# A fused pooled attention and SiLU MLP on one core: a fourth seven-product unit per tile, written into one ordered program

## The chip, the cores and the metric

The kernel runs on one core of a Trainium2 chip. A core has engines that work side by side, each taking its own queue of instructions in order: TensorE (PE in the profile; its weight loads stand apart as PEld), VectorE (DVE), ScalarE (ACT), GpSimd (POOL) and SyncE (SP, which here only issues DMAs). They wait for each other through semaphores. PE writes to PSUM[...]; all other tiles lie in SBUF.

The metric is the device time of one execution in microseconds (us). Of the kernel before there are three timed runs, and one profiled execution whose trace all the views come from.

## What is computed

For 8 batches, 8 heads, 576 positions and head size 64, k and v are averaged over groups of 8 positions, so that each head has 72 keys; q attends to them. The result, 4608 tokens x 512 features, is the input of an MLP with 2048 hidden features.

```python
k_p = k.reshape(B, H, Sp, pool, D).mean(axis=3)
v_p = v.reshape(B, H, Sp, pool, D).mean(axis=3)
scores = scale * np.matmul(q, k_p.transpose(0, 1, 3, 2))
attn = np.exp(scores - max); attn = attn / np.sum(attn, axis=-1)
x = np.matmul(attn, v_p)         # to (4608, 512)
h = x @ w_in                     # (4608, 2048)
g = h * (1.0 / (1.0 + np.exp(-h)))
return g @ w_out                 # (4608, 512)
```

## The kernel before

**Tiles.** The MLP works on 9 tiles t = 0 to 8 of 512 tokens. Each has an up phase (x to h, through SiLU, into h_T: 16 groups g of 128 hidden features x 512 tokens, in bf16) and a down phase (h_T to the output). Attention for batch a = t + 1 (576 tokens) is woven into the phases of tile t, so tiles 0 to 6 carry attention and tiles 7 and 8 don't. x goes to xT, a ring of 2304 tokens: tile 4 crosses its end.

**Plain groups.** plain() (L537, L543) makes one group g with four matmuls over 512 tokens into a bank hp_ps, and ACT applies SiLU on the way to h_T.

**Seven-product units.** A unit y makes four groups at once, as a 2 x 2 block product (two pairs of groups, two halves of 256 tokens) in seven block products instead of eight. UNITS lists the pairs of groups: (4, 6), (8, 10), (12, 14). Each product (L477) is four matmuls of 256 columns. The products are called 2, 5, 1, 4, 3, 7, 6. Products 2, 4 and 7 add up in bank P, 5, 3 and 6 in bank Q, 1 is alone in R. Between them stand (in stage()):

- after 2, ACT copies P to r_sb (L494); after 5, DVE adds Q and r_sb to rr_sb (L497); after 1, DVE subtracts rr_sb from R to t_sb (L500)
- after 4 and after 3, ACT applies SiLU straight from P and from Q (L485)
- after 7, DVE adds P and t_sb to c_sb[0] (L509); after 6, Q and t_sb to c_sb[1] (L512); the stages "h" and "s" are ACT's SiLU of c_sb[0] and c_sb[1] into h_T (L485)

r_sb, rr_sb and t_sb exist once, so the units share them. The products use sums of weight blocks (w_sum1, made once) and of x blocks (x_sum, five DVE additions per tile, L444, made in the down phase of the tile before). In tiles 2 to 8 before the change, groups 4 to 15 are made by the three units and groups 0 to 3 by plain(), in the order of the string THREE, where A is the unit with groups 12 to 15, B that with 4 to 7, C that with 8 to 11.

**Down.** down_quarters() (L645) uses the same scheme once for the whole tile: seven products of 16 matmuls with 256 columns, in banks P, Q, R. Products 2, 5, 1, 7 and 6 take sums of h blocks, h_sum[n] (hidden_sum, DVE, L605), as their stationary operand; products 4 and 3 take h_T itself. A sum's high half needs groups 4 to 7 and 12 to 15, its low half 0 to 3 and 8 to 11. After product 2 ACT copies P to r_sb (L658); after 5 DVE makes rr_sb (L660), after 1 t_sb (L664); 4 is copied by ACT (L666) and 3 by DVE (L671) to o_sb; 7 and 6 are added to t_sb by DVE (L675, L679). Then SP's queue stores o_sb.

**Attention in a tile**: POOL sums k and v rows of batch a (behind a gate that waits for an x sum), PE transposes k (kT_ps), DVE transposes q in four pieces, and for each third of the batch come scores (PE L340, ACT exponential L348), denominators (PE L358, ACT logarithm and exponential L367, L368) and numerators (PE L384, DVE multiply L393 to xT). ACT loads a table set ahead of the exponentials (L400) and another ahead of SiLU (L403).

**Order.** Each engine takes its instructions in the order in which the program issues them. up() and down_quarters() issue the matmuls, and a list of fillers (f_up, f_down) says at which step everything else is put in between (spread()). PSUM: 5 banks of kind "at" (units' P and Q, k transpose, scores, denominators, numerators) and 3 of kind "mm" (units' R, plain groups, the down phase's P, Q, R), each kind handed out in turn.

Of the kernel before, what the change touches and what calls it, by code (L numbers as in the profile page):

```python
# [27 lines left out]
FP32 = mybir.dt.float32  # L28
# [4 lines left out]
ALU = mybir.AluOpType  # L33
# [3 lines left out]
def kernel(  # L37
# [53 lines left out]
    def ps_tile(shape, dtype, tag, name):  # L91
        return psum.tile(shape, dtype, tag=tag, bufs=banks[tag], name=name)
# [24 lines left out]
            singles.tile([128, 5, 2, 256], BF16, name=f"w_sum1{n}") for n in range(2)  # L117
        )
    ]
    x_sum = singles.tile([128, 5, 2, NQ], BF16, name="x_sum")  # L120
    gate = singles.tile([128, 1], BF16, name="gate")
    c_sb = [singles.tile([128, 2, NQ], FP32, name=f"c_sb{n}") for n in range(2)]
# [54 lines left out]
    def load_one(b, name):  # L177
        st = batches.setdefault(b, {})
        raw = raw_tile(f"{name}_raw", H)
        nc.gpsimd.dma_start(out=raw, in_=source(b, name)[:, :, :PH])  # L180
        st[f"{name}_raw"] = raw
# [13 lines left out]
    def behind_x_sums():  # L195
        nc.gpsimd.tensor_copy(out=gate[:1], in_=x_sum[:1, U_XI[6], 0, :1])  # L196

    def pool_k(b):
        pool_rows(kp[:SP], batches[b]["k_raw"])
# [119 lines left out]
    def third(n):  # L319
        return tuple((g, n * QV, (n + 1) * QV) for g in range(2))  # L320
# [78 lines left out]
    def attn_tables():  # L399
        nc.scalar.preload_act_table_set("natural_log_exp_and_others")  # L400
# [13 lines left out]

    UNITS = ((4, 6), (8, 10), (12, 14))
    UW = [
        {
            (i, j): w_in_sb[:, 2 * j : 2 * j + 2, 128 * u : 128 * (u + 2)]  # L420
# [14 lines left out]
    def unit_weight_sum(y, n):  # L435
        a, b = U_W[n]
        nc.vector.tensor_tensor(
            out=w_sum1[y][U_WI[n]], in0=UW[y][a], in1=UW[y][b],
            op=ALU.subtract if n in (6, 7) else ALU.add,
        )  # L440
# [19 lines left out]
    def up(t, fillers, items):  # L460
        step = spread(
            fillers,
            sum(
                KF if len(it) == 3 else 2 * len(it[1].strip("hs")) for it in items
            ),
        )
        ps = {}

        def product(y, n, bank, first):
            if first:  # L470
                tag = "mm" if bank == "R" else "at"
                ps[y, bank] = ps_tile([128, 2, NQ], FP32, tag, f"u_ps{bank}")
            w, x = unit_weights(y, n), unit_x(t, n)
            for u in range(2):
                next(step)
                for kk in range(2):
                    nc.tensor.matmul(  # L477
                        ps[y, bank][:, u, :], lhsT=w[:, kk, 128 * u : 128 * (u + 1)],
                        rhs=x[:, kk, :], start=first and u == 0 and kk == 0,
                        stop=kk == 1, skip_group_check=True,  # L480
                    )

        def hidden(y, i, j, src):
            g = UNITS[y][i]
            nc.scalar.activation(  # L485
                h_T[:, g : g + 2, j * NQ : (j + 1) * NQ], src, func=AF.Silu
            )

        tt = nc.vector.tensor_tensor

        def stage(y, n):
            if n == "2":
                product(y, 2, "P", True)
                nc.scalar.copy(r_sb, ps[y, "P"])  # L494
            elif n == "5":
                product(y, 5, "Q", True)
                tt(out=rr_sb, in0=ps[y, "Q"], in1=r_sb, op=ALU.add)  # L497
            elif n == "1":
                product(y, 1, "R", True)
                tt(out=t_sb, in0=ps[y, "R"], in1=rr_sb, op=ALU.subtract)  # L500
            elif n == "4":
                product(y, 4, "P", False)
                hidden(y, 1, 0, ps[y, "P"])
            elif n == "3":
                product(y, 3, "Q", False)
                hidden(y, 0, 1, ps[y, "Q"])
            elif n == "7":
                product(y, 7, "P", False)
                tt(out=c_sb[0], in0=ps[y, "P"], in1=t_sb, op=ALU.add)  # L509
            elif n == "6":  # L510
                product(y, 6, "Q", False)
                tt(out=c_sb[1], in0=ps[y, "Q"], in1=t_sb, op=ALU.add)  # L512
            elif n == "h":
                hidden(y, 0, 0, c_sb[0])
            else:
                hidden(y, 1, 1, c_sb[1])

        for it in items:
            if len(it) == 3:
                plain(t, step, *it)  # L520
            else:
                for n in it[1]:
                    stage(it[0], n)
        for _ in step:
            pass

    def plain(t, step, g, n0, n):
        tag = "at" if (t, g, n0) == (0, 3, 0) else "mm"
        hp_ps = ps_tile([128, 512], FP32, tag, "hp_ps")
        c0 = (t * NTT + n0) % NX  # L530

        for r0, r1 in ((0, min(n, NX - c0)), (min(n, NX - c0), n)):
            for kk in range(KF) if r1 > r0 else ():
                if r0 == 0:
                    next(step)
                x0 = (c0 + r0) % NX
                nc.tensor.matmul(  # L537
                    hp_ps[:, r0:r1],
                    lhsT=w_in_sb[:, kk, g * 128 : (g + 1) * 128],
                    rhs=xT[:, kk, x0 : x0 + r1 - r0],  # L540
                    start=(kk == 0), stop=(kk == KF - 1),
                )
        nc.scalar.activation(h_T[:, g, n0 : n0 + n], hp_ps[:, :n], func=AF.Silu)  # L543
# [58 lines left out]
    def hidden_sum(n, k0, k1):  # L602
        a, b, op = H_SUMS[n]
        ks = slice(k0, k1)
        nc.vector.tensor_tensor(  # L605
            out=h_sum[n][:, ks, :], in0=quarter(*a, ks), in1=quarter(*b, ks), op=op
        )
# [17 lines left out]
    def left(n, kt, c):  # L625
        cs = slice(128 * c, 128 * (c + 1))
        if n in h_sum:
            return h_sum[n][:, kt, cs]
        i = n - 3
        return h_T[:, i * KQ + kt, i * NQ + 128 * c : i * NQ + 128 * (c + 1)]  # L630
# [55 lines left out]
            pass  # L686


    warm_ps = ps_tile([128, 512], FP32, "mm", "warm_ps")

    def warm_up(n):
# [97 lines left out]
        " C6 Ch Cs g2 g3",  # L789
    )  # L790
    visits = [third(n) for n in range(3)]
    for t in range(NT):
        a = t + 1
        f_up, f_down = [], []
        if t == 0:
            GA = 11
            items = [(g, 0, HS) for g in range(GA)]
            items += [(g, HS, NTT - HS) for g in range(GA)]
            items += [(g, 0, NTT) for g in range(GA, KG)]
            f_up += [(1, lambda: denominators(0, part(0, 1), on_dve=True))]  # L800
            f_up += [(5, lambda: denominators(0, part(1, 1), on_dve=True))]
            f_up += [(13, lambda: numerators(0, part(0, 1)))]
            f_up += [(17, lambda: numerators(0, part(1, 1)))]
        else:
            G = lambda *gs: [(g, 0, NTT) for g in gs]
            if t == 1:
                items = (
                    G(12, 13, 14, 15) + [(0, "25143"), (1, "2"), (0, "7"), (1, "5")]
                    + [(0, "6h"), (1, "1")] + G(0) + [(1, "4"), (0, "s"), (1, "3")] + G(1)
                    + [(1, "7h6")] + G(2) + [(1, "s")] + G(3)  # L810
                )
            else:
                items = []
                for it in THREE[t // B].split():
                    items += [(("BCA".index(it[0])), it[1])] if it[0] in "ABC" else G(int(it[1]))
            if t == 1:
                for n in U_X:
                    f_up.append((0, lambda n=n: unit_x_sum(t, n)))
            for n in (2, 5):
                h_at = 50 if t == B else 54 if t > 1 else 45  # L820
                f_up.append((h_at, lambda n=n: hidden_sum(n, 4, 8)))
            f_up.append((56, lambda: hidden_sum(6, 4, 8)))
            for n, k0 in ((2, 0), (5, 0), (1, 4), (1, 0)):
                f_up.append((64, lambda n=n, k0=k0: hidden_sum(n, k0, k0 + 4)))
            f_down.append((33, lambda: hidden_sum(7, 0, 8)))
            f_down.append((71 if t < B else 50, lambda: hidden_sum(6, 0, 4)))

        for n, t0, f_to, at, parts in (
# [71 lines left out]
        if t == 1:  # L900
            def unit_weight_tiles():
                k_w = big.tile([128, 4, 2, 256], BF16, tag="k_raw2", name="w_sum12")
                v_w = big.tile([128, 4, 2, 256], BF16, tag="v_raw2", name="w_sum12")
                w_sum1.append([k_w[:, i] for i in range(4)] + [v_w[:, 0]])

            f_down.append((72, unit_weight_tiles))
            for i, n in enumerate(U_W):
                f_down.append((73 if i < 2 else 81, lambda n=n: unit_weight_sum(2, n)))
        if t != 1:
            moe_tables()  # L910
        if t == 0:
# [34 lines left out]
```

The softmax here doesn't subtract the row's maximum and nothing guards it: scores larger than these inputs give would overflow.

## Time and profile before

| | |
|---|---|
| three timed runs | 280.13 us median (279.87 to 280.38) |
| the profiled execution | 280.09 us, of which its span is 278.3 |
| PE, DVE, ACT busy over the span | 98%, 79%, 68% |
| h sums (DVE L605), 128x1024 | 64 of 684 ns each |
| unit's DVE additions L497, L500, L509, L512 | 23 each, 682 to 692 ns |
| SiLU from c_sb (ACT L485) | 46 of 629 ns |
| SiLU of a plain group of 512 (ACT L543) | 41 of 593 ns |
| table load (ACT L400, L403) | 17 of 1283 ns |

A line of a timeline has the start, the time it took, the engine and the line of code, what was written from what, the shape, and how many were merged. The time of a matmul in the trace runs on to its modelled end, so the next one starts before it: a 256-column matmul is shown with 273 ns, and four in a row with 0.60 us. On DVE and ACT an instruction can start a little before the one ahead has ended.

### The profile page before, as it was taken

The page shows a single profiled execution, that of the slowest core. Times are in us where ns is not written, and L with a number is a line of the kernel's source. Part 1 is how long each engine was busy: PE and PEld are TensorE (multiplying, and loading weights), DVE is VectorE, ACT ScalarE, POOL GpSimd, SP SyncE. Part 2 cuts the span into 40 slices and gives each one's busy share as a digit, 9 for nine tenths or more (in the row PEclk, how much of TensorE's full clock was granted, in tenths as well). Part 3 has the DMA queues.
Part 4 walks back from the last instruction along what each step waited for, and adds up shares of the span by engine and source line. Part 5 has one row for each costly group of instructions (what it writes and reads, how often), then busy time and mean ns, then how long its engine had stood idle before and what let it go on. Part 6 is the DMA issues. An engine that isn't in the chain of part 4 may idle for free.

```text
span 278.3 us, 7160 instructions
## 1 busy us (share of the span) xinstructions
PE 273.8 (98%) x2877; PEld 204.1 (73%) x2877; DVE 220.8 (79%) x415; ACT 189.3 (68%) x369; POOL 98.5 (35%) x104
## 2 busy tenths in 40 slices
PE   8999999999999999999999999999999999999995
PEld 4448444576778677867888788687877778788784
DVE  4886877788998976897689768986888588966982
ACT  1688767468577966797679757985799578326810
POOL 8745217332148430953086107970640000000001
PEclk9999999999999999999999999999999999999999
DMA  7999999896569879569756835599610041005004
GB/s 209 288 259 240 207 326 182 237 200 109 127 86 212 213 104 174 137 162 138 137 109 176 130 65 133 136 132 138 144 44 2 2 104 49 0 11 138 8 0 152
DMA packets 31314, 37.71 MB, mean 135 GB/s; under 512 B 10353, under 2 KB 22257, under 8 KB 31281
## 3 DMA queue, kind: packets, MB, share of 16 engines
q0 software_dynamic: 23920, 27.03, 51.8%
q1 hardware_dynamic: 6928, 9.58, 12.5%
q10 hardware_dynamic: 432, 0.66, 0.6%
q8 instruction: 22, 0.36, 0.5%
q14 instruction: 12, 0.09, 0.1%
HBM read 36.70 MB, written 9.44 MB: 166 GB/s over the span
## 4 chain that ended last, share of the span: by engine, by line
PE 92%; DVE 3%; ACT 3%; issue 1%
PE o_psQ L645 15%; PE hp_ps L537 15%; PE o_psP L645 15%; PE u_psP L477 11%; PE u_psQ L477 11%; PE o_ps L572 5%; PE o_psR L645 5%; PE sc_ps L340 4%; PE u_psR L477 4%; PE nu_ps L384 3%; PE warm_ps L693 3%; PE den_ps L358 2%; DVE h_sum L605 1%; ACT h_T L543 1%; PE warm_ps L697 1%
## 5 line engine op out<-in xcount | busy, mean ns | idle before, releaser
L645 PEld LDWEIGHTS <-h_sum 128*128 128x128 bf16 x640 | 60.7, 98 | 11.5 <-DVE h_sum L605 1.3
L477 PEld LDWEIGHTS <-w_sum 128*128 128x128 bf16 x460 | 45.0, 98 | 8.1 <-issue 0.2
L605 DVE TENSOR_TENSOR h_sum<-h_T 128x1024 bf16<-128x1024 bf16 (+1 forms) x72 | 49.7, 743 | 1.6 <-ACT h_T L543 1.0
L537 PE MATMUL hp_ps<-xT,w_in_sb 128*128 128x512 bf16 (+3 forms) x268 | 50.3, 332 | 0.0
L348 ACT ACTIVATE es<-sc_ps 72x384 bf16<-72x384 f32 (+1 forms) x100 | 39.1, 470 | 8.5 <-PE sc_ps L340 8.3
L543 ACT ACTIVATE h_T<-hp_ps 128x512 bf16<-128x512 f32 (+2 forms) x63 | 31.7, 520 | 10.0 <-PE hp_ps L537 9.2
L537 PEld LDWEIGHTS <-w_in_sb 128*128 128x128 bf16 x268 | 25.6, 98 | 15.1 <-issue 0.8
L485 ACT ACTIVATE h_T<-c_sb 128x512 bf16<-128x512 f32 x46 | 28.8, 629 | 4.4 <-DVE c_sb L509 3.6
L393 DVE TENSOR_TENSOR xT<-nu_ps,rec 128x384 bf16<-128x384 f32 (+1 forms) x50 | 24.0, 533 | 4.9 <-PE nu_ps L384 4.8
L645 PEld LDWEIGHTS <-h_T 128*128 128x128 bf16 x256 | 24.1, 98 | 4.5 <-issue 0.9
L549 POOL DMA_DIRECT2D out_dram<-o_sb x2 | 1.2, 618 | 67.9 <-issue 67.2
L367 ACT ACTIVATE lnd<-den_ps 128x384 f32<-128x384 f32 (+1 forms) x23 | 11.1, 484 | 19.5 <-PE den_ps L358 19.5
L190 POOL TENSOR_TENSOR raw<-raw 72x1024 f32<-72x1024 f32 x10 | 23.6, 2363 | 0.1
L500 DVE TENSOR_TENSOR t_sb<-u_psR,rr_sb 128x512 f32<-128x512 f32 x23 | 15.9, 692 | 6.7 <-PE u_psR L477 5.0
L494 ACT COPY r_sb<-u_psP 128x512 f32<-128x512 f32 x23 | 13.4, 585 | 10.7 <-PE u_psP L477 8.0
L477 PEld LDWEIGHTS <-w_in_sb 128*128 128x128 bf16 x184 | 17.6, 98 | 2.4
L497 DVE TENSOR_TENSOR rr_sb<-u_psQ,r_sb 128x512 f32<-128x512 f32 x23 | 15.7, 682 | 4.0 <-ACT r_sb L494 2.1
L645 PE MATMUL o_psP<-w_out_sb,h_sum 128*128 128x256 bf16 x128 | 17.6, 273 | 0.0
L512 DVE TENSOR_TENSOR c_sb<-u_psQ,t_sb 128x512 f32<-128x512 f32 x23 | 15.8, 687 | 2.3 <-PE u_psQ L477 2.1
L509 DVE TENSOR_TENSOR c_sb<-u_psP,t_sb 128x512 f32<-128x512 f32 x23 | 15.8, 685 | 1.8 <-PE u_psP L477 0.9
L196 POOL COPY gate<-x_sum 1x1 bf16<-1x1 bf16 x5 | 0.9, 181 | 44.7 <-DVE x_sum L444 44.7
L645 PE MATMUL o_psQ<-w_sum,h_sum 128*128 128x256 bf16 x128 | 16.7, 273 | 0.0
(83 smaller groups left out, 528.2 us busy)
## 6 DMA issues: line engine op xcount, KB each, us to landing
out_dram<-o_sb SPq DMA_DIRECT2D x128, 64.0 KB, 1.7
raw<-in_k_dram POOLq DMA_DIRECT2D x10, 576.0 KB, 8.1
raw<-in_v_dram POOLq DMA_DIRECT2D x10, 576.0 KB, 7.6
q_bf<-in_q_dram POOLq DMA_DIRECT2D x6, 576.0 KB, 10.4
w_in_sb<-in_moe_w_in_dram POOLq DMA_DIRECT2D x8, 256.0 KB, 8.6
w_out_sb<-in_moe_w_out_dram POOLq DMA_DIRECT2D x4, 512.0 KB, 13.2
raw<-in_v_dram POOLq DMA_DIRECT2D x2, 768.0 KB, 10.9
raw<-in_k_dram POOLq DMA_DIRECT2D x1, 768.0 KB, 10.8
```

What stands on the lines that cost most here:

```text
L190: nc.gpsimd.tensor_add(out=raw[:, :, : 2 * D], in0=raw[:, :, : 2 * D], in1=raw[:, :, 2 * D :])
L348: nc.scalar.activation(es[:, s, :], sc[s], func=AF.Exp, scale=score_scale)
L393: nc.vector.tensor_mul(out=xT[:, 2 * g0 + c : 2 * (g0 + ng - 1) + c + 1 : 2, cols], in0=nu[c][:, :w].rearrange("r (g n) -> r g n", g=ng), ...
L477: nc.tensor.matmul(ps[y, bank][:, u, :], lhsT=w[:, kk, 128 * u : 128 * (u + 1)], rhs=x[:, kk, :], start=first and u == 0 and kk == 0, stop ...
L485: nc.scalar.activation(h_T[:, g : g + 2, j * NQ : (j + 1) * NQ], src, func=AF.Silu)
L500: tt(out=t_sb, in0=ps[y, "R"], in1=rr_sb, op=ALU.subtract)
L509: tt(out=c_sb[0], in0=ps[y, "P"], in1=t_sb, op=ALU.add)
L512: tt(out=c_sb[1], in0=ps[y, "Q"], in1=t_sb, op=ALU.add)
L537: nc.tensor.matmul(hp_ps[:, r0:r1], lhsT=w_in_sb[:, kk, g * 128 : (g + 1) * 128], rhs=xT[:, kk, x0 : x0 + r1 - r0], start=(kk == 0), stop= ...
L543: nc.scalar.activation(h_T[:, g, n0 : n0 + n], hp_ps[:, :n], func=AF.Silu)
L605: nc.vector.tensor_tensor(out=h_sum[n][:, ks, :], in0=quarter(*a, ks), in1=quarter(*b, ks), op=op)
L645: nc.tensor.matmul(ps[b][:, c, :], lhsT=left(n, kt, c), rhs=W_OUT[n][:, kt, :], start=b not in begun, stop=kt == k1 - 1, skip_group_check= ...
```

## The change

UNITS gets a fourth entry (0, 2), so that groups 0 to 3 can be made by a unit too; its weight sums (unit 3) are made in tile 2's down phase and lie in spare space and in a new tile w_e. From tile 3 on (T4), run(t) replaces up() and down_quarters(). It goes through PROGRAM, one list of tokens for up and down together; each token issues its instructions on all engines concerned:

- A, B, C, E with 2 5 1 4 3 7 6: a product of the unit with groups 4 to 7, 8 to 11, 12 to 15, 0 to 3; with a or s, its SiLU of c_sb[0] or c_sb[1]
- h and a number with h or l: the high or low half of that h sum (all of 128x1024)
- d and a number: a fourth of a down product's 16 matmuls (for 2, 5 and 1: d2h0, d2h1 with the high half of the sum, d2l0, d2l1 with the low); what follows the product is issued with its last part. o is the addition after product 6
- q0 to q3, k: transposes; sc, de, nu with 0 to 2: scores, denominators, numerators of a third; npp: the numerators of the batch before, last third
- T1, T2: table loads; x and a number: an x sum of the next tile

So product 1 of the down phase, which came whole after 2 and 5, is now in two halves: the high one between the halves of 2 and 5, the low one after 3. The h sums 5h, 2h and 1h lie in the up phase, the others in the down phase. The copy of product 3 moves from DVE to ACT. The x sums stand between the parts of 7 and 6 instead of in one row near the end. In the last tile the down phase is done column half by column half from product 4 on (columns()), with 1's low half in it. In tile 1 the whole sum h_sum 7 is put at step 44 instead of 33 of the down phase; select_v and copy_v (v's cast to vp) stand at 40 and 41.

```diff
--- before.py
+++ after.py
@@ -117,6 +117,7 @@
             singles.tile([128, 5, 2, 256], BF16, name=f"w_sum1{n}") for n in range(2)
         )
     ]
+    w_e = singles.tile([128, 2, 2, 256], BF16, name="w_sum1e")
     x_sum = singles.tile([128, 5, 2, NQ], BF16, name="x_sum")
     gate = singles.tile([128, 1], BF16, name="gate")
     c_sb = [singles.tile([128, 2, NQ], FP32, name=f"c_sb{n}") for n in range(2)]
@@ -414,7 +415,7 @@
 
 
 
-    UNITS = ((4, 6), (8, 10), (12, 14))
+    UNITS = ((4, 6), (8, 10), (12, 14), (0, 2))
     UW = [
         {
             (i, j): w_in_sb[:, 2 * j : 2 * j + 2, 128 * u : 128 * (u + 2)]
...
@@ -685,6 +690,146 @@
         for _ in step:
             pass
 
+
+    def down_stages(t, last):
+        ps = {}
+        bank = {2: "P", 5: "Q", 1: "R", 4: "P", 3: "Q", 7: "P", 6: "Q"}
+        begun = set()
+        add, sub = ALU.add, ALU.subtract
+        tt = nc.vector.tensor_tensor
+        KA = KQ // 2
+
+        def matmuls(n, k0, k1, cs=(0, 1)):
+            b = bank[n]
+            for kt in range(k0, k1):
+                for c in cs:
+                    nc.tensor.matmul(
+                        ps[b][:, c, :], lhsT=left(n, kt, c), rhs=W_OUT[n][:, kt, :],
+                        start=b not in begun,
+                        stop=kt == k1 - 1, skip_group_check=True,
+                    )
+                    begun.add(b)
+
+        def after(n, cc=(0, 1), tail=False):
+            cs = slice(cc[0], cc[-1] + 1)
+            if n == 2:
+                nc.scalar.copy(r_sb, ps["P"])
+            elif n == 5:
+                tt(out=rr_sb, in0=ps["Q"], in1=r_sb, op=add)
+            elif n == 1:
+                tt(out=t_sb[:, cs], in0=ps["R"][:, cs], in1=rr_sb[:, cs], op=sub)
+            elif n == 4:
+                nc.scalar.copy(o_sb[1][:, cs, LO], ps["P"][:, cs])
+                if tail:
+                    store(t, 3, LO, (nc.gpsimd,))
+            elif n == 3:
+                nc.scalar.copy(out=o_sb[0][:, cs, HI], in_=ps["Q"][:, cs])
+                if tail:
+                    store(t, 1, HI)
...
+        def part_of(tok):
+            if tok == "o":
+                return after(6)
+            n = int(tok[1])
+            if not ps:
+                for b in "PQR":
+                    ps[b] = ps_tile([128, 2, CQ], FP32, "mm", f"o_ps{b}")
+            if n in (2, 5, 1):
+                k0 = KA * (tok[2] == "h") + 2 * int(tok[3])
+                matmuls(n, k0, k0 + 2)
+                if tok[2:] == "l1":
+                    after(n)
+            else:
+                k0 = 2 * int(tok[2])
+                matmuls(n, k0, k0 + 2)
+                if k0 + 2 == KQ and n != 6:
+                    after(n)
+
+        def columns(c):
+            for n in (4, 3, 1, 7, 6):
+                matmuls(n, 0, KA if n == 1 else KQ, (c,))
+                after(n, (c,), c == 1)
+
+        return part_of, columns
+
+    PROGRAM = (
+        "q1 A2 A5 q3 A1 C2 q0 A4 C5 A3 B2 C4 A7 A6 Aa C1 C3 As B5 C7 B4 C6 Ca B1 E2 B3 "
+        "Cs h5h E5 B7 E4 h2h B6 E3 Ba E1 E7 Bs k E6 Ea Es h1h T1 npp d2h0 d2h1 h2l d5h0 "
+        "d5h1 h5l q2 d1h0 sc0 h7l h6h d1h1 h6l d2l0 d2l1 d5l0 sc1 de0 d5l1 h1l d40 h7h "
+        "d41 d42 d43 sc2 de1 d30 d31 d32 d33 d1l0 nu0 de2 nu1 d1l1 x7 T2 d70 x6 d71 x4 "
+        "d72 x3 d73 x1 d60 d61 d62 d63 o "
+    )
+
+    def run(t):
+        a = t + 1
+        attn, last = a < B, t == NT - 1
+        stage = unit_stages(t, iter(int, 1))
+        part_of, columns = down_stages(t, last)
+        toks = PROGRAM.split()
+        attn_toks = ("T1 T2 k npp q0 q1 q2 q3 sc0 sc1 sc2 de0 de1 de2 nu0 nu1").split()
+        if last:
+            i = toks.index("d40")
+            sums = [x for x in toks[i:] if x[0] == "h"]
+            toks = toks[:i] + sums + ["L0", "L1"]
+        toks = [x for x in toks if attn or x not in attn_toks]
+        if a == B - 1:
+            toks.insert(1 + max(toks.index("de2"), toks.index("nu1"), toks.index("o")), "nu2")
+        if t == T4:
+            toks.insert(0, "T2")
+        if attn:
+            if a + 1 < B - 1:
+                load_q(a + 1)
+            behind_x_sums()
+            pool_k(a)
+            if a + 1 < B:
+                load_one(a + 1, "k")
+            pool_v(a)
+            if a + 1 < B:
+                load_one(a + 1, "v")
+                if a + 1 == B - 1:
+                    load_q(a + 1)
+                load_rest(a + 1, "k")
+                load_rest(a + 1, "v")
+        for x in toks:
+            if x[0] in "ABCE" and x[1] in "2514376as":
+                stage("ABCE".index(x[0]), {"a": "h"}.get(x[1], x[1]))
+            elif x[0] == "L":
+                columns(int(x[1]))
...
+            elif x[0] == "h":
+                k0 = 4 if x[2] == "h" else 0
+                hidden_sum(int(x[1]), k0, k0 + 4)
...
+            elif not last:
+                unit_x_sum(t + 1, int(x[1]))
 
     warm_ps = ps_tile([128, 512], FP32, "mm", "warm_ps")
 
@@ -789,8 +934,12 @@
         " C6 Ch Cs g2 g3",
     )
     visits = [third(n) for n in range(3)]
+    T4 = 3
     for t in range(NT):
         a = t + 1
+        if t >= T4:
+            run(t)
+            continue
         f_up, f_down = [], []
         if t == 0:
             GA = 11
@@ -822,7 +971,7 @@
             f_up.append((56, lambda: hidden_sum(6, 4, 8)))
             for n, k0 in ((2, 0), (5, 0), (1, 4), (1, 0)):
                 f_up.append((64, lambda n=n, k0=k0: hidden_sum(n, k0, k0 + 4)))
-            f_down.append((33, lambda: hidden_sum(7, 0, 8)))
+            f_down.append((33 if t > 1 else 44, lambda: hidden_sum(7, 0, 8)))
             f_down.append((71 if t < B else 50, lambda: hidden_sum(6, 0, 4)))
 
         for n, t0, f_to, at, parts in (
@@ -902,10 +1051,14 @@
                 k_w = big.tile([128, 4, 2, 256], BF16, tag="k_raw2", name="w_sum12")
                 v_w = big.tile([128, 4, 2, 256], BF16, tag="v_raw2", name="w_sum12")
                 w_sum1.append([k_w[:, i] for i in range(4)] + [v_w[:, 0]])
+                w_sum1.append([v_w[:, 1 + i] for i in range(3)] + [w_e[:, i] for i in range(2)])
 
             f_down.append((72, unit_weight_tiles))
             for i, n in enumerate(U_W):
                 f_down.append((73 if i < 2 else 81, lambda n=n: unit_weight_sum(2, n)))
+        if t == 2:
+            for i, n in enumerate(U_W):
+                f_down.append((76 + 2 * i, lambda n=n: unit_weight_sum(3, n)))
         if t != 1:
             moe_tables()
         if t == 0:
```

More of the change, by code (lines that the diff above doesn't have):

```diff
@@ L466, in up, with unit_stages @@
         )
+        stage = unit_stages(t, step)
+        for it in items:
+            if len(it) == 3:
+                plain(t, step, *it)
+            else:
+                for n in it[1]:
+                    stage(it[0], n)
+        for _ in step:
+            pass
+    def unit_stages(t, step):
         ps = {}
@@ L516, in stage @@
                 hidden(y, 1, 1, c_sb[1])
[L518 to L525, printed above, removed]
+        return stage
     def plain(t, step, g, n0, n):
@@ L686, in down_quarters @@
             pass
+    def down_stages(t, last):
[31 more added lines that the diff above has]
+                    store(t, 1, HI)
+            elif n == 7:
+                tt(out=o_sb[0][:, cs, LO], in0=ps["P"][:, cs], in1=t_sb[:, cs], op=add)
+                for c in cc:
+                    store(t, c, LO if tail else FULL, (nc.scalar if tail else nc.sync,))
+            else:
+                tt(out=o_sb[1][:, cs, HI], in0=ps["Q"][:, cs], in1=t_sb[:, cs], op=add)
+                for c in cc:
+                    if tail:
+                        store(t, 3, HI, both)
+                    else:
+                        store(t, 2 + c, FULL, (nc.gpsimd if last else nc.sync,))
+        def part_of(tok):
[10 more added lines that the diff above has]
+                    after(n)
+            else:
+                k0 = 2 * int(tok[2])
[7 more added lines that the diff above has]
+        return part_of, columns
@@ new lines @@
+    PROGRAM = (
[5 rows of a table added]
+    )
[34 more added lines that the diff above has]
+                columns(int(x[1]))
+            elif x[:2] == "de":
+                denominators(a, visits[int(x[2])])
+            elif x[0] in "do":
+                part_of(x)
+            elif x[0] == "h":
+                k0 = 4 if x[2] == "h" else 0
+                hidden_sum(int(x[1]), k0, k0 + 4)
+            elif x == "T1":
+                attn_tables()
+            elif x == "T2":
+                moe_tables()
+            elif x == "k":
+                k_transpose(a)
+            elif x == "npp":
+                numerators(a - 1, visits[2])
+            elif x[0] == "q":
+                n = int(x[1])
+                q_transpose(a, n % 2, n // 2)
+            elif x[:2] == "sc":
+                scores(a, visits[int(x[2])])
+            elif x[:2] == "nu":
+                numerators(a, visits[int(x[2])])
+            elif not last:
+                unit_x_sum(t + 1, int(x[1]))
```

## Prediction

> **What bounds the kernel now.** I read four views. The page comes first, then the stretches of single tiles, then the timelines of TensorE and VectorE inside one tile, and last the list of waits.
>
> The first part of the page has PE busy for nearly the whole span, with the chain that ended last on it:
>
> ```profile
> span 278.3 us, 7160 instructions
> PE 273.8 (98%) x2877; PEld 204.1 (73%) x2877; DVE 220.8 (79%) x415; ACT 189.3 (68%) x369; POOL 98.5 (35%) x104
> ...
> PE 92%; DVE 3%; ACT 3%; issue 1%
> ```
>
> [...] So I checked the starts. In PE's timeline at the head of tile 3, the columns are start, length, and instructions:
>
> ```profile
> 112.39 0.60 PE L477 MATMUL u_psR<-x_sum,w_sum 128*128 128x256 bf16 x4
> 112.83 0.60 PE L477 MATMUL u_psQ<-x_sum,w_in_sb 128*128 128x256 bf16 x4
> ...
> 120.81 1.89 PE L537 MATMUL hp_ps<-xT,w_in_sb 128*128 128x512 bf16 x8
> 122.54 0.38 PE L645 MATMUL o_psP<-w_out_sb,h_sum 128*128 128x256 bf16 x2
> ```
>
> Four 256-column matmuls start every 0.437 us, so 0.109 us each. Eight of 512 columns take 122.54-120.81 = 1.73 us, or 0.216 each. [...] Starts follow at these steps through tiles 2 to 8: PE waits for nobody there. The tile stretches (length, then busy of PE, PEld, DVE, ACT, POOL) say how near the others are; tile 3, tile 7, and tile 8 with the tail:
>
> ```profile
> 109.78:138.51 28.73, 28.73 (x326) 22.64 (x324) 23.31 (x42) 22.12 (x43) 12.68 (x10) 1.00 0.71 144
> 225.31:250.18 24.87, 24.87 (x215) 20.62 (x212) 20.41 (x35) 13.01 (x23) 0.00 (x0) 1.00 0.14 36
> 250.18:278.30 28.12, 25.03 (x214) 20.52 (x211) 18.43 (x31) 11.53 (x22) 1.24 (x2) 1.00 0.26 76
> ```
>
> DVE has 5.4 us of slack in a tile with attention, ACT 6.6. What matters is where in the tile DVE's slack lies. Its timeline behind the third unit:
>
> ```profile
> 117.34 0.69 DVE L497 TENSOR_TENSOR rr_sb<-u_psQ,r_sb 128x512 f32<-128x512 f32 x1
> 117.95 0.68 DVE L509 TENSOR_TENSOR c_sb<-u_psP,t_sb 128x512 f32<-128x512 f32 x1
> 118.55 0.68 DVE L512 TENSOR_TENSOR c_sb<-u_psQ,t_sb 128x512 f32<-128x512 f32 x1
> 119.33 0.69 DVE L500 TENSOR_TENSOR t_sb<-u_psR,rr_sb 128x512 f32<-128x512 f32 x1
> 120.16 0.69 DVE L509 TENSOR_TENSOR c_sb<-u_psP,t_sb 128x512 f32<-128x512 f32 x1
> 121.08 0.69 DVE L512 TENSOR_TENSOR c_sb<-u_psQ,t_sb 128x512 f32<-128x512 f32 x1 [0.23 <-PE u_psQ L477]
> 121.69 4.29 DVE L605 TENSOR_TENSOR h_sum<-h_T 128x1024 bf16<-128x1024 bf16 x7
> ```
>
> Independent adds start 0.60 apart (117.34, 117.95, 118.55); the seven h sums 0.60 too ((4.29-0.69)/6). But an add that overwrites or reads what the one just ahead of it used starts 0.78 later (t_sb after c_sb, 118.55 to 119.33) or 0.83 (c_sb after t_sb, 119.33 to 120.16), though PE's inputs were there. I price these at 0.79 and 0.82. [...]
>
> **The saving, part by part.** Four plain groups are 16 matmuls x 0.216 = 3.45 us. The unit is 7 products x 0.437 = 3.06. PE saves 0.40 in each of tiles 3 to 8, and 0.44 in tile 4, whose plain groups are split where xT wraps (32 x 0.109 = 3.49).
>
> Attention's small matmuls take some back. In tile 3 now, a block between full-size matmuls costs 0.093 to enter and 0.011 to leave, beside its work: scores 0.47, numerators 0.44 alone or 0.77 for two in a row, denominators 0.17, and 0.10 where denominators turn to scores. Five blocks sum to 3.75 us. The new order has five too: npp; sc0; sc1 de0; sc2 de1; nu0 de2 nu1. The pair of numerators is split (+0.11), and there is one more turn between scores and denominators (+0.10; the direction isn't in the trace, so 0 to 0.2). Sum 3.97, so 0.22 back, and 0.18 net is left in tiles 3 to 6. Tiles 7 and 8 have no attention and keep 0.40.
>
> Edits that I cost at nothing: the o_sb copy goes from DVE to ACT, whose slack is above. The five weight sums in tile 2 (0.34 each) lie in DVE's two holes of 1.05 and 1.11 us around the o_sb copy. POOL's and SP's queues keep their order; the x sums earlier only open POOL's gate sooner, and kp is wanted later than before. If that cover failed, each would be late by its own length.
>
> One gain in tile 1: h_sum 7 (1.2 us) goes from step 33 behind the vp copies. Now the copies wait for it, and PE waits for them: denominators to numerators take 0.32 instead of 0.17, and a hole of 0.32 instead of 0.07 follows. That is 0.40 us back.
>
> **What DVE does to it.** I walk one tile from the start of A2 (time 0), in program order, with the intervals above. The products end on PE at multiples of 0.437. DVE starts 0.25 to 0.27 behind the last product (c_sb at 114.85, its product ended 114.58). A7 is the tenth product, so it ends at 4.37 and c_sb of A starts at 4.64; DVE idles just before it, so nothing earlier matters. From there DVE's queue is
> c7A c6A tC rrB c7C c6C tB h5h rrE c7B h2h c6B tE c7E c6E h1h,
> and each has its inputs before DVE is free. Of its 15 intervals, three are c6 to t (0.79), tC to rrB and tE to c7E are 0.82, ten are 0.60: 6.00 + 2.37 + 1.64 = 10.01. So h1h ends at 4.64 + 10.01 + 0.69 = 15.34.
>
> PE alone would want it sooner. d1h0 is due after 28 products (12.22), kT (0.13), npp (0.56) and d2h, d5h (1.75): 14.66. The weights of d1 are h_sum itself, so their load can begin only behind h1h, and a matmul starts some 0.11 after its load. With 0.06 for the wake (vp ended at 73.33, the waiting load began at 73.39) that is 15.50. PE loses 0.84. Part of this shows sooner, at E3: rrE ends at 10.73, E3 is due at 10.48, and it overwrites the bank that rrE reads; this 0.3 is inside the 0.84.
>
> Next, d2l0 wants h2l. Behind h1h stand npp's two multiplies (0.60 + 0.47 + 0.47), so h2l starts at 16.19, ends at 16.87 and serves PE at 17.04. PE is there at 15.50 + 0.44 + 0.57 + 0.44 = 16.95: 0.09 more. Then d5l0 (h5l ends 17.47, due 17.91), sc1, d40 (its r_sb copy, behind the table load and four exponentials, ends at 18.8, due 19.6) and d30 are in time. DVE catches up under d4, d3, d7 and d6, so the lag isn't handed on. A tile with attention: -0.18 + 0.93 = +0.75, four of them +3.0, tile 4's wrap -0.04.
>
> Tiles 7 and 8 have neither npp nor kT under which DVE could catch up: d1h0 is due at 13.97 and served at 15.50, so 1.53 lost and 0.40 saved, +1.13 each. In tile 8 the first column needs product 3's bank at 18.99, while rr_sb stands behind h7l, h6h and h6l and ends at 19.17, which adds 0.24.
>
> Sum: -0.40 + 3.0 - 0.04 + 1.13 + 1.37 = +5.06. The profiled execution took 280.09 us (span 278.3 and 1.8 around it), 0.04 below the median of 280.13. Forecast: 285.1 us, span 283.4.
>
> **Bounds.** A dependent interval can't be under 0.60, as independent ones aren't; with all five at 0.60 h1h ends at 14.33. If the waiting loads cost PE nothing beyond DVE's end, 0.1 a tile goes. The turn of scores to denominators moves the sum by 0.4 either way. A third of the dependent intervals hidden would leave some 283.2[...].
>
> **Rivals.**
> - DVE keeps up (0.12). If the dependent intervals don't recur, h1h ends at 14.33, before 14.66, and attention tiles run at PE's rate; a small wait in tiles 7 and 8 could be absorbed. Then -0.40 - 4 x 0.18 - 0.04 - 2 x 0.40 = -1.96, so 278.1 us. For it: DVE's total, 25.4 of 28.6 us a tile, fits. Against: the intervals are seen at each such pair. It decides from a chain 0.85 us shorter than mine.
> - The two effects cancel within each other's error (0.07), near 280.1: the waits shrink to some 0.3 us a tile.
> - ACT becomes the bound besides (0.10). It takes 16 activations of 0.49 and four copies of 0.48 in 12.4 us, then a 1.28 us table load ahead of the exponentials; Es ends at 15.41, the first exponential starts at 16.7, and the bank of sc1 and r_sb hang on it. If that comes a microsecond later, PE waits 0.7 in four tiles: 288 us.
> - My forecast, DVE's chain holding PE back (0.71), with its own range of 282.5 to 286.5.
>
> A difference under 0.2% (0.56 us) can't be told from none here. Faster: 0.12 and a little of the cancelling case, 0.13. Same: 0.06. Slower: 0.81. The range from 281.2 to 286.8 leaves out the faster case and most of the ACT case.
>
> **What would show it.** In tiles 3 to 6 PE has a hole near E3 (0.3) and one ahead of d1h0 (0.5), with DVE h_sum or rr_sb named as releaser, and the period from tile to tile is 29.5 instead of 28.7. DVE runs without a hole from A7 to h6l. Tile 7 takes 26.0 instead of 24.9. In tile 1 the holes at numerators are gone. If the holes aren't there and the period is 28.5, DVE's chain is wrong; if PE waits for ACT, the third rival is right.

## The result and the profile after

The changed kernel takes 293.46 us median (293.30 to 295.46, six runs) against 280.07 for the kernel before: a ratio of 1.0489, 95% interval 1.0461 to 1.0517. The forecast was slower too, but by 5.1 us; it is 13.4, and 293.46 lies above the range, which ended at 286.8.

The page of the changed kernel, in its first part and its chain that ended last (shares by engine):

```profile
span 291.5 us, 7335 instructions
PE 274.8 (94%) x2923; PEld 208.7 (72%) x2933; DVE 239.8 (82%) x443; ACT 194.4 (67%) x381; POOL 99.0 (34%) x104
...
PE 64%; DVE 16%; DMA 12%; issue 4%; POOL 2%; ACT 1%; DVEq 0%; POOLq 0%
```

DVE is now 16% of the chain instead of 3%. The stretches of tiles 3 to 8 (length, then busy of PE, PEld, DVE, ACT, POOL, the granted clock, DMA share and GB/s) show where:

```profile
109.12:138.80 29.68, 28.97 (x339) 23.62 (x336) 25.59 (x47) 23.61 (x45) 13.80 (x12) 1.00 0.72 145
138.80:170.47 31.67, 29.04 (x338) 23.55 (x336) 27.39 (x46) 22.96 (x44) 12.09 (x10) 1.00 0.51 109
170.47:202.15 31.68, 29.05 (x339) 23.54 (x337) 27.40 (x46) 22.96 (x44) 17.46 (x18) 1.00 0.84 129
202.15:236.03 33.88, 31.25 (x354) 24.60 (x352) 28.04 (x49) 23.17 (x44) 6.58 (x4) 0.95 0.13 32
236.03:261.96 25.93, 24.81 (x229) 21.83 (x225) 21.39 (x37) 12.87 (x23) 0.00 (x0) 1.00 0.17 42
261.96:291.50 29.54, 25.12 (x226) 21.71 (x223) 20.35 (x34) 13.19 (x25) 1.23 (x2) 1.00 0.24 72
```

Against the kernel before, tile by tile:

| tile | before | after | difference | forecast |
|---|---|---|---|---|
| 1 | 30.21 | 29.80 | -0.41 | -0.40 |
| 2 | 28.73 | 28.74 | 0 | 0 |
| 3 | 28.73 | 29.68 | +0.95 | +0.75 |
| 4 | 28.78 | 31.67 | +2.89 | +0.71 |
| 5 | 28.73 | 31.67 | +2.94 | +0.75 |
| 6 | 29.29 | 33.88 | +4.59 | +0.75 |
| 7 | 24.87 | 25.93 | +1.06 | +1.13 |
| 8, to the end | 28.15 | 29.51 | +1.36 | +1.37 |

(The start of tile 1 moved by -0.26 besides. In two kernels of like code up to there, this one and that of the first run below, the start of tile 3 differs by 0.19.) Tiles 1, 7 and 8 came as worked out, tile 3 nearly. What is missing, some 8.2 us, lies in tiles 4, 5 and 6. In tiles 4 and 5 DVE is busy 1.8 us longer than in tile 3, with about the same instructions (46 and 47). The list of waits names it:

```profile
PEld L489 <- DVE x_sum L445: 7.4, 3, 2.5
PE u_psR L489 <- DVE x_sum L445: 6.6, 3, 2.2
```

Three times, PE is idle for 2.2 us until an x sum is made. Now the end of tile 3 and the head of tile 4, first DVE, then POOL, then PE (start, length):

```profile
136.86 3.71 DVE L445 TENSOR_TENSOR x_sum<-xT 128x512 bf16<-128x512 bf16 x4
140.50 0.68 DVE L730 TENSOR_TENSOR o_sb<-o_psP,t_sb 128x512 f32<-128x512 f32 x1
141.10 0.88 DVE L445 TENSOR_TENSOR x_sum<-xT 128x512 bf16<-128x512 bf16 x1
```

```profile
137.67 0.32 POOL L197 COPY gate<-x_sum 1x1 bf16<-1x1 bf16 x1 [9.25 <-DVE x_sum L445]
137.95 2.33 POOL L191 TENSOR_TENSOR raw<-raw 72x1024 f32<-72x1024 f32 x1
140.36 1.33 POOL L194 TENSOR_TENSOR kp<-raw 72x512 bf16<-72x512 f32 x1
```

```profile
139.24 0.60 PE L489 MATMUL u_psQ<-xT,w_sum 128*128 128x256 bf16 x4
142.04 0.61 PE L489 MATMUL u_psR<-x_sum,w_sum 128*128 128x256 bf16 x4 [2.20 <-DVE x_sum L445]
```

Four x sums took 1.42 us in a run shown below; here they take 3.71. The second of the new order, that for product 6, opens POOL's gate, and POOL's first addition runs from 137.95 to 140.28. The fourth x sum, that for product 3, is held: it takes 2.71 us instead of 0.42 and ends at 140.57, 0.29 behind POOL. The last x sum, that for product 1, meets POOL's second addition (to 141.70) and ends at 141.98, 0.28 behind. The first product 1 of the tile needs that sum. It was due at 139.68 and starts at 142.04, so PE loses 2.36 us.

Ahead of tiles 5 and 6 the same two sums take 2.71 and 0.88 us again, and end 0.29 and 0.28 us behind POOL's additions. Which of the two was first at work the trace doesn't show: the record has the held sum at the end of tile 3 start at 137.86, 0.09 us ahead of POOL's addition, but neighbouring sums overlap on DVE by 0.08 us there.

In the kernel before, the gate opened on the sum made last, and this kept the two apart. Here are the five x sums at the end of tile 2, then POOL:

```profile
109.14 1.76 DVE L444 TENSOR_TENSOR x_sum<-xT 128x512 bf16<-128x512 bf16 x5
110.97 0.18 POOL L196 COPY gate<-x_sum 1x1 bf16<-1x1 bf16 x1 [8.98 <-DVE x_sum L444]
111.11 2.35 POOL L190 TENSOR_TENSOR raw<-raw 72x1024 f32<-72x1024 f32 x1
```

In the trace before, no x sum and no h sum overlaps one of these additions of POOL; all 40 x sums take 0.41 to 0.42 us.

Tile 6 has the same wait and loses 1.65 us more. Stretches of tile 6, with the granted clock behind POOL:

```profile
203.00:205.90 2.90, 0.70 (x7) 0.47 (x6) 2.90 (x5) 0.37 (x1) 2.82 (x3) 1.00 0.11 28
206.20:209.60 3.40, 3.40 (x19) 2.43 (x17) 2.72 (x6) 1.57 (x3) 2.60 (x2) 0.50 0.54 136
209.70:213.00 3.30, 3.30 (x33) 2.95 (x31) 1.98 (x3) 2.54 (x6) 0.00 (x0) 1.00 0.53 134
```

Behind the idle stretch PE gets half the clock for 3.4 us: 19 matmuls instead of 33. Why only here is taken up in the last section.

### The profile page after: what moved, and what is told of

Read it like the earlier page. It is cut to its first block, busy times and chain, and to the rows that moved or that the text cites. A ratio compares the mean times of both kernels' runs of the same rounds, so it can differ in the third digit from the quotient of the medians.

```text
span 291.5 us, 7335 instructions
## 1 busy us (share of the span) xinstructions
PE 274.8 (94%) x2923; PEld 208.7 (72%) x2933; DVE 239.8 (82%) x443; ACT 194.4 (67%) x381; POOL 99.0 (34%) x104
## 4 chain that ended last, share of the span: by engine, by line
PE 64%; DVE 16%; DMA 12%; issue 4%; POOL 2%; ACT 1%; DVEq 0%; POOLq 0%
PE u_psP L489 9%; PE o_psQ L706 9%; PE o_psP L706 9%; PE u_psQ L489 8%; DMA w_in_sb<-in_moe_w_in_dram 6%; DMA w_out_sb<-in_moe_w_out_dram 5%; PE o_psR L706 4%; DVE c_sb L524 4%; PE o_psP L650 4%; PE o_psQ L650 4%; PE hp_ps L542 3%; DVE h_sum L610 3%; PE u_psR L489 3%; PE sc_ps L341 3%; DVE t_sb L512 3%
## 5 line engine op out<-in xcount | busy, mean ns | idle before, releaser
L489 PEld LDWEIGHTS <-w_sum 128*128 128x128 bf16 x532 | 52.1, 99 | 15.0 <-DVE x_sum L445 7.4
L706 PEld LDWEIGHTS <-h_sum 128*128 128x128 bf16 x480 | 44.8, 98 | 12.9 <-DVE h_sum L610 5.5
L497 ACT ACTIVATE h_T<-c_sb 128x512 bf16<-128x512 f32 x58 | 36.3, 629 | 11.3 <-DVE c_sb L521 11.0
L489 PEld LDWEIGHTS <-w_in_sb 128*128 128x128 bf16 x232 | 22.9, 99 | 5.5 <-issue 2.2
L542 PE MATMUL hp_ps<-xT,w_in_sb 128*128 128x512 bf16 (+2 forms) x151 | 25.9, 317 | 0.3
L489 PE MATMUL u_psR<-x_sum,w_sum 128*128 128x256 bf16 x116 | 17.4, 273 | 6.6 <-DVE x_sum L445 6.6
L445 DVE TENSOR_TENSOR x_sum<-xT 128x512 bf16<-128x512 bf16 x40 | 22.7, 624 | 0.0
L509 DVE TENSOR_TENSOR rr_sb<-u_psQ,r_sb 128x512 f32<-128x512 f32 x29 | 19.6, 678 | 3.6 <-ACT r_sb L506 2.1
L512 DVE TENSOR_TENSOR t_sb<-u_psR,rr_sb 128x512 f32<-128x512 f32 x29 | 19.9, 686 | 3.1 <-PE u_psR L489 0.5
L548 ACT ACTIVATE h_T<-hp_ps 128x512 bf16<-128x512 f32 (+2 forms) x39 | 18.1, 476 | 5.8 <-PE hp_ps L542 4.8
L497 ACT ACTIVATE h_T<-u_psQ 128x512 bf16<-128x512 f32 x29 | 17.3, 595 | 5.2 <-PE u_psQ L489 5.0
L542 PEld LDWEIGHTS <-w_in_sb 128*128 128x128 bf16 x156 | 14.6, 98 | 8.5 <-issue 0.7
L489 PE MATMUL u_psQ<-x_sum,w_in_sb 128*128 128x256 bf16 x116 | 18.0, 277 | 1.2 <-DVE rr_sb L509 0.4
```

Of the source, the lines that this page charges most:

```text
L445: nc.vector.tensor_tensor(out=x_sum[:, U_XI[n]], in0=x_quarter(t, *a), in1=x_quarter(t, *b), op=ALU.subtract if n in (3, 4) else ALU.add,)
L489: nc.tensor.matmul(ps[y, bank][:, u, :], lhsT=w[:, kk, 128 * u : 128 * (u + 1)], rhs=x[:, kk, :], start=first and u == 0 and kk == 0, stop ...
L497: nc.scalar.activation(h_T[:, g : g + 2, j * NQ : (j + 1) * NQ], src, func=AF.Silu)
L542: nc.tensor.matmul(hp_ps[:, r0:r1], lhsT=w_in_sb[:, kk, g * 128 : (g + 1) * 128], rhs=xT[:, kk, x0 : x0 + r1 - r0], start=(kk == 0), stop= ...
L706: nc.tensor.matmul(ps[b][:, c, :], lhsT=left(n, kt, c), rhs=W_OUT[n][:, kt, :], start=b not in begun, stop=kt == k1 - 1, skip_group_check= ...
```

## The experiments

Six kernels, each beside the kernel before on the same chip.

**The gate on the last sum.** The name of the sum that the gate reads becomes an argument; in tiles 4 to 6 it is 1.

```diff
-    def behind_x_sums():
-        nc.gpsimd.tensor_copy(out=gate[:1], in_=x_sum[:1, U_XI[6], 0, :1])
+    def behind_x_sums(n=6):
+        nc.gpsimd.tensor_copy(out=gate[:1], in_=x_sum[:1, U_XI[n], 0, :1])
...
-            behind_x_sums()
+            behind_x_sums(1 if t > T4 else 6)
```

> The changed kernel, with POOL's gate on the x sum that is now made last (1) instead of 6. Theory P (POOL's additions, let in between the x sums, hold up the next x sum[...]): no x sum longer than 0.45 us, PE's wait of 2.36 us at the first product 1 of tiles 4, 5 and 6 is gone, and with it the stretch of half clock in tile 6; 293.46 - 3 x 2.36 - 1.7 = 284.7 us, tiles 3 to 6 at 29.3 to 29.7 us. Rival Q (the x sum waits in DVE's own queue, because it now stands between the additions of products 7 and 6): one x sum stays at 2.7 us, 293 us.

Measured: 284.83 us, ratio to before 1.0172 (1.0155 to 1.0189). The x sums at the end of tile 3, and the stretches of tiles 4, 5 and 6:

```profile
137.04 1.42 DVE L445 TENSOR_TENSOR x_sum<-xT 128x512 bf16<-128x512 bf16 x4
138.37 0.69 DVE L730 TENSOR_TENSOR o_sb<-o_psP,t_sb 128x512 f32<-128x512 f32 x1
138.97 0.42 DVE L445 TENSOR_TENSOR x_sum<-xT 128x512 bf16<-128x512 bf16 x1
```

```profile
138.98:168.28 29.30, 28.86 (x338) 23.64 (x336) 24.62 (x47) 23.18 (x44) 11.92 (x9) 1.00 0.59 118
168.28:197.59 29.31, 28.88 (x339) 23.63 (x337) 24.63 (x47) 23.18 (x44) 17.30 (x17) 1.00 0.94 137
197.59:227.43 29.84, 29.40 (x354) 23.83 (x351) 25.16 (x48) 23.18 (x44) 7.36 (x5) 1.00 0.16 38
```

8.6 us are back by one operand of one copy, the half clock of tile 6 is gone (1.00 instead of 0.95), and the places of the x sums between the additions of 7 and 6 cost nothing. What is left, +4.9 us, is near the forecast's +5.06; how far for the right reasons is looked at below.

**The gate on the first sum, in the kernel before.**

```diff
-        nc.gpsimd.tensor_copy(out=gate[:1], in_=x_sum[:1, U_XI[6], 0, :1])
+        nc.gpsimd.tensor_copy(out=gate[:1], in_=x_sum[:1, U_XI[4], 0, :1])
```

> The kernel before, with nothing changed but POOL's gate, which reads the x sum made first (4) instead of the one made last (6). Theory P: in tiles 2 to 6 one of the later x sums takes 2.7 us instead of 0.42, and the additions behind it come 2.3 us late; PE loses 1.5 to 2.3 us in each of five tiles, 287.5 to 291.5 us, and perhaps a stretch of half clock besides. Rival Q: the x sums stand in a row here, so nothing happens, 280.1 us.

Measured: 300.47 us, ratio 1.0732 (1.0716 to 1.0748). The direction is theory P's, the size is 9 us above the end of its range. DVE, then POOL, at the end of tile 2:

```profile
113.73 5.12 DVE L444 TENSOR_TENSOR x_sum<-xT 128x512 bf16<-128x512 bf16 x5
```

```profile
114.49 2.34 POOL L190 TENSOR_TENSOR raw<-raw 72x1024 f32<-72x1024 f32 x1
116.90 1.33 POOL L193 TENSOR_TENSOR kp<-raw 72x512 bf16<-72x512 f32 x1
```

Two sums are held, one behind each of POOL's additions, so the five take 5.12 us instead of 1.76, 3.4 late and not 2.3. PE waits 2.7 us in tiles 2 to 5 and 4.8 in tile 6. Half the clock for a while follows in some of them: the granted clock is 0.95 over tile 2 (33.09 us), 1.00 over tile 3 (31.42) and 0.983 over the whole run, where the changed kernel, with one such stretch of 3.41 us, has 0.994. My estimate from these is three stretches: 0.017 x 298.8 = 5.1 us of clock, 1.7 each. In tile 6 a third sum is held, behind POOL's next addition. I had allowed for one held sum and at most one stretch at half clock.

**Two pairs of rr_sb and t_sb.** On top of the gate's repair, the units take turns.

```diff
+    spare = h_sum[6].rearrange("p k n -> p (k n)").bitcast(FP32).rearrange(
+        "p (b c n) -> p b c n", b=2, c=2
+    )
+    unit_rt = ((rr_sb, t_sb), (spare[:, 0], spare[:, 1]))
...
         def stage(y, n):
+            rr_sb, t_sb = unit_rt[(0, 0, 1, 1)[y] if t >= T4 else 0]
```

> The run with the gate on the last x sum, and the units of tiles 3 to 8 taking turns between two pairs of rr_sb and t_sb (the second pair lies in h_sum 6, idle in the up phase). Theory D (DVE's chain from c_sb of A to h_sum 1 holds PE back, and 0.19 to 0.22 us of it at four places is the wait of an addition that overwrites what the one ahead of it reads): the four places start 0.60 apart, h_sum 1 ends 0.8 us sooner, PE's waits ahead of E3 and d1h0 are gone in tiles 3 to 6 and 0.75 instead of 1.44 in tiles 7 and 8; 284.7 - 4 x 0.8 - 2 x 0.75 = 280.0 us. Rival (0.79 is what such an addition takes anyhow): 284.7 us.

Measured: 281.25 us, ratio 1.0044 (1.0029 to 1.0059): 3.6 of the expected 4.7 us. First the run with the gate alone, where t_sb overwrites what c_sb reads and rr_sb what t_sb reads:

```profile
144.22 0.68 DVE L524 TENSOR_TENSOR c_sb<-u_psQ,t_sb 128x512 f32<-128x512 f32 x1
145.01 0.69 DVE L512 TENSOR_TENSOR t_sb<-u_psR,rr_sb 128x512 f32<-128x512 f32 x1
145.84 0.69 DVE L509 TENSOR_TENSOR rr_sb<-u_psQ,r_sb 128x512 f32<-128x512 f32 x1
```

The same place with two pairs (the second is named h_sum after its memory):

```profile
144.18 0.68 DVE L530 TENSOR_TENSOR c_sb<-u_psQ,t_sb 128x512 f32<-128x512 f32 x1
144.78 0.68 DVE L518 TENSOR_TENSOR h_sum<-u_psR,h_sum 128x512 f32<-128x512 f32 x1
145.38 0.68 DVE L515 TENSOR_TENSOR rr_sb<-u_psQ,r_sb 128x512 f32<-128x512 f32 x1
```

0.79 and 0.83 become 0.60 and 0.60, so the dependence is the cause. PE's wait at E3 is gone in tiles 4 to 6, that ahead of d1h0 falls from 0.45 to 0.24 or less there and from 1.13 to 0.69 in tiles 7 and 8. Tile 3 kept 29.47 us: its first h sum met one of POOL's additions and took 1.49 us instead of 0.68. In tiles 4 and 5 it met one too (0.91 and 0.92 us), in tile 6 not; there the wait ahead of d1h0 is gone, in 4 and 5 it is the 0.24. The run that is put together shows such a case.

**Plain groups again.** The gate's repair, the new order, but groups 0 to 3 by plain() in tiles 3 to 8.

```diff
-        "q1 A2 A5 q3 A1 C2 q0 A4 C5 A3 B2 C4 A7 A6 Aa C1 C3 As B5 C7 B4 C6 Ca B1 E2 B3 "
-        "Cs h5h E5 B7 E4 h2h B6 E3 Ba E1 E7 Bs k E6 Ea Es h1h T1 npp d2h0 d2h1 h2l d5h0 "
+        "q1 A2 A5 g0 q3 A1 C2 q0 A4 C5 A3 B2 C4 A7 A6 Aa C1 C3 As B5 C7 B4 C6 Ca B1 B3 g1 "
+        "Cs h5h B7 h2h B6 Ba Bs g2 k g3 h1h T1 npp d2h0 d2h1 h2l d5h0 "
...
+            elif x[0] == "g":
+                plain(t, iter(int, 1), int(x[1]), 0, NTT)
```

> The run with the gate on the last x sum, and groups 0 to 3 made by plain() again in tiles 3 to 8, with the rest of the new order kept. Theory D: without the fourth unit's four additions DVE keeps up; no wait of PE at product 3 or d1h0; tiles 3 to 6 take 28.73 + 0.22 for the split numerators and the second turn of scores to denominators = 28.95 us, tiles 7 and 8 are within 0.3 us of the kernel before; with 0.40 won in tile 1, 280.5 us. Rival (the new order of the down phase makes waits by itself): 282 us or more, with waits ahead of d1h0.

Measured: 281.32 us, ratio 1.0046 (1.0031 to 1.0061), 0.8 us above the figure and below the rival's. Tiles 3 and 5 take 28.85 us: PE waits nowhere there, and the new order's attention costs 0.12 over before, half of the 0.22 that I had worked out. Tiles 7 and 8 miss their figure, at +0.52 and +0.67. Tile 7:

```profile
237.91 1.04 PE L706 MATMUL o_psP<-w_out_sb,h_sum 128*128 128x256 bf16 x8
239.29 1.03 PE L706 MATMUL o_psQ<-w_out_sb,h_sum 128*128 128x256 bf16 x8 [0.34 <-ACT h_T L548]
```

Here PE waits for ACT's SiLU of a plain group, whose bank the down phase takes next; in my order it stands behind the SiLU of c_sb. That is a fault of this kernel's order, not of the change.

**A version put together.** The program in tiles 4 to 6 only, the gate's repair, two pairs, and some tokens moved (the gate and the pairs are as in the runs above).

```diff
-    T4 = 3
+    T4, T5 = 4, B - 1
...
-        if t >= T4:
+        if T4 <= t < T5:
...
-        "Cs h5h E5 B7 E4 h2h B6 E3 Ba E1 E7 Bs k E6 Ea Es h1h T1 npp d2h0 d2h1 h2l d5h0 "
-        "d5h1 h5l q2 d1h0 sc0 h7l h6h d1h1 h6l d2l0 d2l1 d5l0 sc1 de0 d5l1 h1l d40 h7h "
-        "d41 d42 d43 sc2 de1 d30 d31 d32 d33 d1l0 nu0 de2 nu1 d1l1 x7 T2 d70 x6 d71 x4 "
+        "Cs h5h E5 B7 E4 B6 E3 Ba E1 h2h E7 Bs k E6 Ea Es h1h T1 npp d2h0 d2h1 h2l d5h0 "
+        "d5h1 h5l q2 d1h0 sc0 h7l h6h d1h1 h6l d2l0 d2l1 d5l0 de0 sc1 d5l1 h1l d40 h7h "
+        "d41 d42 d43 de1 sc2 d30 d31 d32 d33 d1l0 de2 nu0 nu1 d1l1 x7 T2 d70 x6 d71 x4 "
```

> A version put together from what the runs showed: the new program only in tiles 4 to 6 (tile 3 begins without its late gate, tiles 7 and 8 have no attention to hide DVE's lag under), the gate on the last x sum, two pairs of rr_sb and t_sb, h2h put between t_sb and c_sb of the fourth unit, denominators ahead of the next scores and numerators 0 and 1 side by side. Theory D: no wait of PE at E3 or d1h0, the blocks of attention at 3.75 us or less, so tiles 4 to 6 at 28.3 to 28.5 instead of 28.73 to 29.29; with 0.40 won in tile 1, 280.0 - 0.4 - 1.0 = 278.6 us (278.2 to 279.2). Rival (the new order costs PE something besides DVE's lag and the x sums): tiles 4 to 6 stay at 28.7 or more, 279.6 us or more.

Measured: 280.46 us, ratio 1.0013 (1.0007 to 1.0020): the rival's side. Tiles 4, 5 and 6 take 29.42, 28.88 and 29.29 us, no better than 28.78, 28.73 and 29.29 before. In tile 4, DVE and POOL:

```profile
146.82 1.49 DVE L616 TENSOR_TENSOR h_sum<-h_T 128x1024 bf16<-128x1024 bf16 x1
148.23 0.68 DVE L515 TENSOR_TENSOR h_sum<-u_psQ,r_sb 128x512 f32<-128x512 f32 x1
```

```profile
146.49 1.27 POOL L194 TENSOR_TENSOR vp<-raw 72x512 bf16<-72x512 f32 x1
```

The first h sum, with two inputs from SBUF as an x sum has, is held to 148.31 by POOL's addition that ends at 147.76; PE then waits 0.57 at E3. The other expectation that fell is attention at 3.75 us. The five blocks of tile 4 sum to 4.0, against 3.7 in the kernel before. Counted from where the next full-size matmul was due to where it starts, the block of denominators with two numerators took 1.17 us where such a block took 1.03 before (0.91 for nu0 nu1 where 0.77 was expected). And one third's denominators moved from a block with numerators to one with scores: the two blocks take 0.54 and 0.84 us where they took 0.70 and 0.56, 0.12 more. So in tiles with attention this order gives back some 0.3 of the unit's 0.40 before any wait.

**One edit alone, in the kernel before:** h_sum 7 of tile 1 later.

```diff
-            f_down.append((33, lambda: hidden_sum(7, 0, 8)))
+            f_down.append((33 if t > 1 else 44, lambda: hidden_sum(7, 0, 8)))
```

> The kernel before with one edit of the change alone: the whole h_sum 7 of tile 1 at step 44 of the down phase, behind the copies of v, instead of step 33. The prediction's step: PE's two waits at numerators in tile 1 go, 0.36 to 0.40 us, 279.6 us; nothing else moves. Rival (the sum put later holds up product 7 of tile 1): 280.0 us or more.

Measured: 279.58 us, ratio 0.9983 (0.9975 to 0.9990). Tile 1 takes 29.80 instead of 30.21 us, the others are the same. By 0.17%, this is faster than the kernel before, and it is the fastest of all the kernels here.

## Why the prediction was wrong

**The step that failed** stands among the edits that I cost at nothing: "the x sums earlier only open POOL's gate sooner". I asked whether kp would be late and not what POOL's additions do to the sums still to come. Measured, it costs 3 x 2.36 us of PE's waiting in tiles 4 to 6 and 1.65 us at half clock, 8.7 together; the changed kernel and the run with its gate on the last sum differ by 8.6. The rule that "if that cover failed, each would be late by its own length" failed with it: what comes late is an x sum, which is wanted sooner than kp, and it is late by about the length of POOL's instruction (2.29 us against 2.33). Tile 3 was spared, as its x sums are made by tile 2 in the old order; tiles 7 and 8, as there is nothing to pool.

**The rest holds in its mechanism, with two terms too large.** In the run with the gate on the last sum, the forecast's walk can be read against the trace of tile 4, which starts at 138.98:

- c_sb of A was put at 4.64 and starts at 143.62, so 4.64. h_sum 1 was to end at 15.34 and ends at 154.33, so 15.35:

```profile
153.65 0.68 DVE L610 TENSOR_TENSOR h_sum<-h_T 128x1024 bf16<-128x1024 bf16 x1
```

- d1h0 was put at 15.50 and starts at 15.41, with the releaser named. The wake of 0.06 was right; the 0.11 between a weight load and its matmul isn't there behind a wait (load and matmul both start at 154.39 here, at 156.58 in the changed kernel), so each of tiles 3 to 8 was put 0.09 too high:

```profile
154.39 0.61 PE L706 MATMUL o_psR<-w_sum,h_sum 128*128 128x256 bf16 x4 [0.29 <-DVE h_sum L610]
```

- E3 waits 0.31 (0.3). Tiles 7 and 8 cost +1.06 and +1.37 (+1.13, +1.37). Tile 3 lost 0.2 more than worked out: its first h sum took 0.96 us instead of 0.68 at the end of one of POOL's additions, and E3 waited 0.59. That is the same collision, in small.
- Attention's new blocks were put at 0.22 a tile. The run with plain groups gives 0.12, the price of the second turn. The pair of numerators, put at +0.11 for being split, cost nothing: with denominators between the two the block takes 1.03 us, as before. So tiles 4 to 6 lose some 0.55 each there and not 0.71 to 0.75. That 284.83 stands so near to 285.1 is in part luck, as tile 3 erred the other way.
- Tile 1: -0.41, forecast -0.40, and alone -0.45 in the timed runs.
- Of the rivals, none was right. ACT is named in none of the waits that matter. "DVE keeps up" falls with the third run, where even without four of the five dependent intervals tiles 7 and 8 still wait 0.69.

## What to carry to other kernels

When an instruction is a gate, ask what it keeps apart, not only what it lets start: here one copy that read the second sum instead of the last cost two thirds of the loss. Before DVE work is added to a phase, walk DVE's queue through that phase with the measured intervals, dependent pairs at their own price; a total that fits over the whole tile says nothing of the place where PE waits. A saving of 0.40 us on an engine without gaps is lost to a single wait or a few more changes between kinds of matmul.

## What the runs showed of the hardware

- Additions on DVE with two SBUF inputs that met one of POOL's additions ended behind it: in the changed kernel the x sums by 0.28 to 0.29 us (2.71 and 0.88 us instead of 0.42) and an h sum of tile 3 by 0.55 (0.96 instead of 0.68), in the version put together an h sum by 0.55 (1.49 instead of 0.68), so a little less than their own length. Additions with one input from PSUM were not lengthened: in the kernel before, 49 of them (L497, L500, L509, L512, L679) overlap POOL's additions, and each took 0.65 to 0.69 us. Once POOL's addition was the longer one: in tile 6 of the changed kernel it starts at 205.01, while the last x sum still runs (to 205.33), and takes 2.53 us instead of the 2.38 of tiles 4 and 5.
- An fp32 addition of 512 columns on DVE that read or overwrote what the one ahead wrote or read started 0.79 to 0.83 us behind it, an independent one 0.60 (the two timelines at the run with two pairs).
- In the changed kernel the granted clock is 0.50 from 206.22 to 209.63 us, for 3.41 us, and 1.00 just before and behind it. The length of the wait alone didn't decide it: PE lost 2.36 us at the same place in tiles 4 and 5, and the clock there is 1.00. In the run with the gate on the first sum, PE is idle for 2.63 us in each of tiles 2 and 3, and the clock is 0.95 over the one and 1.00 over the other.
- What set tile 6 apart is only an estimate. The changed kernel's trace has four entries of the clock, which begin at 4.83, 206.22, 209.63 and 291.55 us: 201.39, 3.41 and 81.92 apart, so 59, 1 and 24 times 3.413. If they lie on a grid of that step, tile 6's wait (203.02 to 205.38) falls within one step, the one ahead of the half clock, and the waits of tiles 4 and 5 fall across a border (1.68 and 0.68, 0.74 and 1.63). No run moved a wait against such a grid to try it.
